# Three more Strassen units, a shared gather and a later first fold in a fused spectral and MLP kernel

## The chip, the cores and the metric

The kernel runs on one core of one Trainium2 chip. The metric is the device time of one execution in microseconds (us). An engine is named as the profile names it: PE is TensorE (PEld its weight loads), DVE is VectorE, ACT is ScalarE, POOL is GpSimd, SP is SyncE, which issues the DMAs.

## The reference

Input x is 2048 tokens of 448 features, all in float32. The output is a sum of three things: x, a spectral filter of the normalised x, and an MLP block with token shifts on the normalised x.

```python
def _A_ref(x, w_r, w_i):
    X = jnp.fft.rfft2(x, axes=(-2, -1)) * (w_r + 1j * w_i)
    return jnp.fft.irfft2(X, s=(S, D), axes=(-2, -1))

def _B_ref(x, w1, w2, w3, w4):
    h = _gelu(_layernorm(x, axis=-1) @ w1)        # 448 x 448
    # four quarters of h shifted by +1, -1, +2, -2 tokens, joined again
    x1 = x + shifted(h) @ w2                      # 448 x 448
    return x1 + _gelu(_layernorm(x1, axis=-1) @ w3) @ w4   # 448 x 1792, 1792 x 448

xn = _layernorm(A_x, axis=-1)
return A_x + _A_ref(xn, A_w_r, A_w_i) + _B_ref(xn, B_w1, B_w2, B_w3, B_w4)
```

## The kernel before

Every operand is split into a high and a low float16 part, and each product is three passes (high x high, high x low, low x high), named PASS. The 2048 tokens are 16 blocks of 128 (b = 0 to 15), kept in eight tiles xt of two blocks.

The first part of the kernel (up to about 100 us) normalises, multiplies by w1 and w2 and prepares w3 and w4. The rest consists of three kinds of work:

- The last two matrices, w3 and w4, run over eight groups of two blocks (G = 0 to 7) and seven units each (fp = 0 to 6, 256 hidden features a unit). `front` (matmuls on L384, tile pw) multiplies a unit by w3, 22 matmuls of 256 columns; ACT and DVE apply the gelu and split the result into tile hf (L704, L706, L707). `back` (L785, tile acc) multiplies it by w4, 12 matmuls of 448 columns, accumulated over the units of a group. L792 adds a finished accumulator to xt. `mlp` orders fronts and backs: a front runs one or two units ahead of its back.
- The spectral part: `do_fold` (L516 on ACT, L522 to L525 on POOL) and `step1` (L532, L533, PE on L542, tile ps) for every block; then 16 chunks (`chunk_a`, `chunk_b`, `chunk_z`, `chunk_c`: tiles pp, px, z, pu, PE on L600, L617, L645); then `gather_u` (L658), which copies the chunks' results Y1 into U for eight blocks at a time, four copies for the high and four for the low part; then `inv_a` (tile pe, L666) and `inv_b` (tile py, L687, L689) for every block.
- Units by Strassen's products. In groups 6 and 7, the units listed in SEVEN use seven products of half-size blocks (224 columns) in place of eight: `sums` makes the sums of the activations (tiles g and hz, L716 to L723), `w4_sums` those of w4 (L735, split by L267 and L268, into w4t), and `seven` issues 7 x 3 matmuls (L756) into the group's accumulators and two further PSUM banks, tile side. At the end of the group five DVE operations (L764) add the side banks to xt.

All of it is issued through a scheduling layer that orders the instructions of each engine by priority and by a modelled timeline. The groups are filler for the spectral part: groups 1 and 2 run beside the folds, 3 and 4 beside the chunks, 4 and 5 beside the inverse. Explicit ties hold some work behind other work: FOLD names, for each pair of blocks, the unit behind whose activation its fold stands on ACT, PACE the unit behind whose `back` the pair's step1 stands on PE, EARLY the units behind which the DMA and rescaling of earlier rows (`unscale`) are put, and LATE the units behind which the w4 sums stand.

PSUM tiles come from rotating pairs of banks by tag: mm for the fronts, acc for the accumulators, tr for pp and pe, sp for ps, px, pu and py. A tile must be read out before its bank is used again.

Of the kernel before, what the change touches and what calls it, by code (L numbers as in the profile page):

```python
# [15 lines left out]
AF = mybir.ActivationFunctionType  # L16
# [4 lines left out]
NB, NC = 16, 16  # L21
# [8 lines left out]
VPRE = 2.0 ** -3  # L30
EPS = 1e-5
AH = 2
PACE = [(0, 6), (1, 1), (1, 2), (1, 4), (1, 5), (2, 0), (2, 1), (2, 3)]
FOLD = [(0, 5), (1, 0), (1, 1), (1, 3), (1, 4), (1, 6), (2, 0), (2, 2)]
PIN = [("a3",), ("a3",), ("a3",), ("a3",)]
WMAX = [(1, 4), (1, 5), (1, 6), (2, 0), (2, 1), (2, 2), (2, 3), (2, 4)]
HS = 3
EVAC, FILL = 0, 100000
DH = D // 2
SEVEN = {6: [0, 1, 2, 3, 4, 5], 7: [0, 1, 2, 4, 5]}  # L40
ORD = {G: list(range(7)) for G in range(6)} | {6: list(range(7)), 7: [0, 1, 2, 4, 5, 3, 6]}

ME = [0, 224] + list(range(2, 224, 2))
MO = list(range(1, 224, 2))
# [78 lines left out]
def body(tc, nc, x, wf, w1, w2, w3, w4, c_g, c_n, c_small, out):  # L123
    V, A, P, T, SY = nc.vector, nc.scalar, nc.gpsimd, nc.tensor, nc.sync
    PSUM = bass.MemoryType.PSUM

    @contextlib.contextmanager
    def prio(base):
        kept = tc.cur_priority
        tc.cur_priority = max(base, at.get(base, 0))  # L130
        yield
        at[base] = tc.cur_priority
        tc.cur_priority = kept
# [19 lines left out]
    def bank(tag, name):  # L153
        return ps.tile([128, 512], F32, tag=tag, bufs=2, name=name)
# [106 lines left out]
    def split_w(hi, lo, src, s, low=None):  # L261
        if low is P:
            P.tensor_scalar(out=src, in0=src, scalar1=s, scalar2=0.0, op0=ALU.mult, op1=ALU.add)
            i = A.activation(out=hi, in_=src, func=AF.Copy)
            j = P.tensor_tensor(out=lo, in0=src, in1=hi, op=ALU.subtract)
            return i.ins, j.ins
        i = A.activation(out=hi, in_=src, func=AF.Copy, scale=s)  # L267
        j = V.scalar_tensor_tensor(out=lo, in0=src, scalar=s, in1=hi, op0=ALU.mult, op1=ALU.subtract)  # L268
        return i.ins, j.ins
# [88 lines left out]
    @contextlib.contextmanager  # L358
    def behind(*key):
        key = key if len(key) > 1 else key[0]  # L360
        with contextlib.ExitStack() as st:
            for i in after[key]:
                st.enter_context(tc.issue_after(i))
            yield
# [127 lines left out]
    def unscale(p, part):  # L492
        t = part.rearrange("p (b n) -> p b n", b=2)
        SY.dma_start(t, xv[:, 2 * p:2 * p + 2])
        return lambda: V.scalar_tensor_tensor(out=xt[p], in0=xt[p], scalar=p12, in1=t, op0=ALU.mult, op1=ALU.add)
# [14 lines left out]
    def do_fold(b0):  # L510
        X = pfd.tile([128, 2, D + 1], F32, tag="xf", bufs=3, name=f"xf{b0}")
        after["X", b0] = (SY.dma_start(X[:, :, 0:D], xv[:, b0:b0 + 2]).ins,)
        with behind("f", *FOLD[b0 // 2]):
            for i in range(2):
# [137 lines left out]
    U, vhs = {}, {}  # L652

    def gather_u(b0):
        U[b0] = [pv.tile([128, 4, 8, 128], F16, tag=f"U{p}", bufs=1, name=f"U{b0}{p}") for p in range(2)]
        for p in range(2):
            for q in range(4):
                V.tensor_copy(out=U[b0][p][:113, q].rearrange("p b (c k) -> p b c k", c=NC),  # L658
                              in_=Y1[:113, p, q, :, b0:b0 + 8].rearrange("p c b k -> p b c k"))

    def inv_a(b):
        pe = bank("tr", f"pe{b}")
# [29 lines left out]
    acc, hs = {}, {}  # L692

    def front(G, fp, tag):
# [5 lines left out]
        with prio(EVAC):  # L700
            if fp in SEVEN.get(G, ()):
                hs[G, fp] = sums(G, fp, pm)
# [24 lines left out]
    def w4_sums(j, part):  # L727

        t = part.rearrange("p (k n) -> p k n", n=DH)
        SY.dma_start(t.rearrange("p (f k) n -> p f (k n)", f=2), w4v[:, 2 * j:2 * j + 2])  # L730

        def go():
            for o, i, k, op in ((3, 3, 1, ALU.subtract), (1, 1, 0, ALU.subtract),
                                (0, 3, 0, ALU.add), (2, 2, 0, ALU.subtract)):
                V.tensor_tensor(out=t[:, o], in0=t[:, i], in1=t[:, k], op=op)  # L735
            split_w(w4t[j][:, 0], w4t[j][:, 1], t, s4)
        return go

    side = {}

    def seven(G, fp):
        h = hs.pop((G, fp))
        lead, last = fp == SEVEN[G][0], fp == SEVEN[G][-1]
        if lead:
            side[G] = [bank("sp" if G == 7 else "tr", f"side{G}{i}") for i in range(2)]
        m1, m6, m5, m7 = (side[G][i][:, DH * k:DH * k + DH] for i in range(2) for k in range(2))
        a2, a1 = acc[G][0], acc[G][1]
        a12 = acc[G][2][:, 0:DH] if G == 7 else a1[:, DH:D]
        w = lambda f, k: [w4p[0][:, i, 2 * fp + f, DH * k:DH * k + DH] for i in range(2)]
        t2, t1, t4, t3 = ([w4t[fp][:, i, k] for i in range(2)] for k in range(4))  # L750
        begins = fp == ORD[G][0]
        for blk, to, b, new in ((2, m1, w(0, 0), lead), (4, a1[:, 0:DH], w(1, 0), begins), (1, a2[:, 0:DH], t4, begins),
                                (6, a12, w(1, 1), begins and G == 7), (5, m5, t1, lead), (3, m6, t2, False),
                                (0, m7, t3, False)):
            for n, (hi, wi) in enumerate(PASS):
                m = T.matmul(to, h[:, hi, 128 * blk:128 * blk + 128], b[wi], start=new and n == 0,  # L756
                             stop=last and n == 2 and blk in (2, 5, 3, 0), skip_group_check=True)
        after["m", G, fp] = (m.ins,)
        if last:
            x = xt[G].rearrange("p b (k n) -> p (b k) n", k=2)  # L760
            wide = lambda m, n: m.unsqueeze(1).to_broadcast([128, n, DH])
            for to, m in ((x, wide(m1, 4)), (x[:, 0:2], wide(m6, 2)), (x[:, 3], m6), (x[:, 1:4:2], wide(m5, 2)),
                          (x[:, 0:2], wide(m7, 2))):
                V.scalar_tensor_tensor(out=to, in0=m, scalar=p34[:, 1:2], in1=to, op0=ALU.mult, op1=ALU.add)  # L764

    def back(G, fp):
        first, end = fp == ORD[G][0], fp == ORD[G][-1]
        if first:
            acc[G] = [bank("acc", f"acc{G}{i}") for i in range(2)]
            if G == 7:  # L770
                acc[G].append(bank("tr", "acc72"))
        if fp in SEVEN.get(G, ()):
            seven(G, fp)
            return
        h = hs.pop((G, fp))
        for i in range(2):
            b = 2 * G + i
            c = D // 2 if b == NB - 1 else D
            parts = [(slice(o, o + c), acc[G][i + o // c][:, 0:c]) for o in range(0, D, c)]
            for r, to in parts:  # L780
                with behind("m", G, fp) if G == 7 and end and ("m", G, fp) in after else contextlib.nullcontext():
                    for f in (2 * fp, 2 * fp + 1):
                        for n, (hi, wi) in enumerate(PASS):
                            o = 256 * (f % 2) + 128 * i
                            m = T.matmul(to, h[:, hi, o:o + 128], w4p[0][:, wi, f, r],  # L785
                                         start=first and f % 2 == 0 and n == 0, stop=end and f % 2 == 1 and n == 2,
                                         skip_group_check=G in SEVEN)
                after["m", G, fp] = (m.ins,)
            if end:
                with prio(EVAC):  # L790
                    for r, to in parts:
                        V.scalar_tensor_tensor(out=xb(b)[:, r], in0=to, scalar=p34[:, min(G, 1):min(G, 1) + 1],  # L792
                                               in1=xb(b)[:, r], op0=ALU.mult, op1=ALU.add)
                        if G > 4:
                            SY.dma_start(ov[:, b, r], xb(b)[:, r])

    def mlp(Gs, hook=None, ahead=1, tags=("mm",)):
        with prio(FILL):
            todo = [(G, fp) for G in Gs for fp in ORD[G]]
            done = 0  # L800
# [169 lines left out]
    Y1 = Y.rearrange("p i q c (b k) -> p i q c b k", k=8)  # L970
# [2 lines left out]
    for i in range(4):  # L973
        P.memset(xh_buf[i][:, 904:], 0.0)
    loads = stage("loads", 1808, 0)
    EARLY = {(1, 0): 1, (1, 1): 2, (1, 3): 3, (1, 5): 4, (1, 6): 5, (2, 1): 6, (2, 2): 7}

    def between(G, fp):
        if (G, fp) in EARLY:
            p = EARLY[G, fp]  # L980
            go = unscale(p, loads[:, 896 * (p % 2):896 * (p % 2) + 896])
            with behind("f", G, fp):
                go()

    mlp([1, 2], hook=between, ahead=AH, tags=("mm", "tr"))
    for b in range(0, NB, 2):
        do_fold(b)
        step1_in(b)
        step1_in(b + 1)
        with behind("m", *PACE[b // 2]):  # L990
            step1(b)
# [24 lines left out]
    for n in range(17):  # L1016
# [4 lines left out]
        if n:  # L1021
            b = bs[n - 1]
# [2 lines left out]
                finish(b)  # L1025
    close("pa2")
    pz = pool("pz")
    LATE = [(0, 5, 4), (1, 5, 5), (2, 5, 6), (3, 6, 0), (4, 6, 1), (5, 6, 3)]

    def w4_late(G, fp):  # L1030
        for n, (j, *at) in enumerate(LATE):
            if at == [G, fp]:
# [32 lines left out]
```

## Time and profile before

| | |
|---|---|
| median of 3 runs | 412.83 us (412.76 to 412.90) |
| the profiled execution | 412.93 us |
| its span, first to last instruction | 411.1 us |
| granted PE clock | 1.000 |
| PE matmul busy | 404.9 us, 98% of the span, 3382 matmuls |
| DVE busy | 329.5 us, 80% |
| ACT busy | 256.0 us, 62% |
| POOL busy | 96.8 us, 24% |
| DMA moved | 51.28 MB |

Busy time of PE is modelled at the matmuls' ends, so gaps between starts are the better measure. A row of the groups has: line, engine, operation, tiles written and read, shapes, count; then busy time in us and the mean of one in ns; then the engine's idle time before them and what ended it. A row of the timeline has: start in us from the span's start, length in us, engine, line, operation, tiles, count, and in brackets an idle time ahead of it with what ended it.

### The profile page before, as it was taken

How to read it: one execution, taken by the hardware profiler on the slowest of the kernel's cores; microseconds unless marked ns; L12 is line 12 of the kernel's file. 1: busy time of each engine (PE TensorE's matmuls, PEld its weight loads, DVE VectorE, ACT ScalarE, POOL GpSimd, SP SyncE). 2: the span in 40 equal slices, each digit the busy share in tenths (PEclk: the TensorE clock that was granted, in tenths of full speed). 3: DMA queues.
4: the chain of work that ended last, by engine and by line, in shares of the span. 5: the costliest groups of instructions: out<-in, count | busy, mean ns of one | idle time of the engine just before them, and what ended most of it. 6: DMA issues, size and time to landing. Idle time of an engine off the chain costs nothing.

```text
span 411.1 us, 8687 instructions
## 1 busy us (share of the span) xinstructions
PE 404.9 (98%) x3382; PEld 296.8 (72%) x3382; DVE 329.5 (80%) x675; ACT 256.0 (62%) x434; POOL 96.8 (24%) x172
## 2 busy tenths in 40 slices
PE   8999999999999999999999999999999999999996
PEld 3655555765658777777888887877776767998995
DVE  4888999898867879854798888967999978986645
ACT  4688879973757876544589887854344443653431
POOL 3877720101344947400022111110000000000000
PEclk9999999999999999999999999999999999999999
DMA  8959979914966557215256756510111043210101
GB/s 276 351 190 180 152 150 317 177 62 89 175 171 202 156 199 224 86 52 138 62 144 152 176 153 156 132 27 2 47 67 69 2 136 112 69 46 0 46 2 45
DMA packets 56168, 51.28 MB, mean 125 GB/s; under 512 B 37632, under 2 KB 50496, under 8 KB 56128
## 3 DMA queue, kind: packets, MB, share of 16 engines
q1 hardware_dynamic: 56128, 50.74, 46.6%
q8 instruction: 26, 0.43, 0.4%
q14 instruction: 14, 0.11, 0.1%
HBM read 38.28 MB, written 3.67 MB: 102 GB/s over the span
## 4 chain that ended last, share of the span: by engine, by line
PE 65%; DVE 13%; ACT 8%; issue 6%; DMA 5%; POOL 2%; SPq 1%; POOLq 0%; DVEq 0%; ACTq 0%
PE pw L384 26%; PE acc L785 19%; PE side L756 3%; PE ps L542 3%; PE pw L413 2%; PE pe L666 2%; PE acc L756 2%; PE py L687 2%; ACT te L622 2%; DVE xt L455 1%; PE pu L645 1%; DMA x2mem<-w 1%; PE pp L600 1%; DVE y L487 1%; PE px L617 1%
## 5 line engine op out<-in xcount | busy, mean ns | idle before, releaser
L384 PE MATMUL pw<-x2mem,w3p 128*128 128x256 f16 x1232 | 151.3, 273 | 0.0
L384 PEld LDWEIGHTS <-w3p 128*128 128x128 f16 x1232 | 119.2, 98 | 21.7
L785 PE MATMUL acc<-w4p,hf 128*128 128x448 f16 (+1 forms) x552 | 112.7, 348 | 0.6 <-DVE hf L707 0.6
L785 PEld LDWEIGHTS <-hf 128*128 128x128 f16 x552 | 53.5, 98 | 40.5 <-DVE hf L707 1.0
L704 ACT ACTIVATE pw<-pw,pe 128x512 f32<-128x512 f32 x45 | 29.4, 654 | 35.6 <-PE pw L384 35.4
L707 DVE SCALAR_TENSOR_TENSOR hf<-pw,h,hf 128x512 f16<-128x512 f32 x45 | 33.5, 746 | 15.2 <-ACT hf L706 14.9
L453 PE MATMUL pw<-w2p,h 112*128 112x448 f16 x192 | 39.9, 352 | 0.8 <-DMA h<-hs 0.8
L413 PE MATMUL pw<-w1p,xT 128*128 128x448 f16 x176 | 35.4, 352 | 0.0
L626 POOL TENSOR_TENSOR z<-te 128x450 f32<-128x450 f32 x16 | 15.7, 981 | 69.5 <-DVE te L624 69.5
L706 ACT ACTIVATE hf<-pw,h 128x512 f16<-128x512 f32 x45 | 30.7, 685 | 1.1
L453 PEld LDWEIGHTS <-h 112*128 112x128 f16 x192 | 18.7, 98 | 17.2 <-DMA h<-hs 1.0
L413 PEld LDWEIGHTS <-xT 128*128 128x128 f16 x176 | 17.0, 98 | 16.4 <-DVE xT L378 0.8
L607 ACT ACTIVATE pf<-pp 64x450 f16<-64x450 f32 x32 | 17.3, 542 | 12.6 <-DVE pf L608 8.3
L608 DVE TENSOR_TENSOR pf<-pp,pf 64x450 f16<-64x450 f32 x32 | 19.9, 622 | 4.3 <-ACT pf L607 3.9
L756 PEld LDWEIGHTS <-hz 128*128 128x128 f16 x231 | 22.2, 98 | 0.2
L722 ACT ACTIVATE hz<-g,h 128x896 f16<-128x896 f32 x11 | 11.5, 1041 | 14.3 <-DVE g L719 14.3
L622 ACT ACTIVATE te<-px 64x450 f32<-64x450 f32 x32 | 17.3, 539 | 1.1 <-PE px L617 0.6
L525 POOL TENSOR_TENSOR f<-xr 128x452 f32<-128x452 f32 x16 | 17.7, 1128 | 0.6
L533 DVE TENSOR_TENSOR xh<-f,xh 128x452 f16<-128x452 f32 x16 | 12.6, 829 | 5.5 <-ACT xh L532 5.5
L723 DVE SCALAR_TENSOR_TENSOR hz<-g,h,hz 128x896 f16<-128x896 f32 x11 | 12.6, 1150 | 5.1 <-ACT hz L722 4.9
L522 POOL TENSOR_TENSOR xr<-xf 128x452 f32<-128x452 f32 x8 | 9.4, 1179 | 25.9 <-issue 20.4
L532 ACT ACTIVATE xh<-f 128x452 f16<-128x452 f32 x16 | 8.4, 571 | 10.0 <-POOL f L525 10.0
(180 smaller groups left out, 688.4 us busy)
## 6 DMA issues: line engine op xcount, KB each, us to landing
wc<-wf SPq DMA_DIRECT2D x32, 225.0 KB, 3.8
wl<-wf SPq DMA_DIRECT2D x8, 450.0 KB, 3.7
xt<-x SPq DMA_DIRECT2D x8, 448.0 KB, 8.2
xf<-x SPq DMA_DIRECT2D x8, 448.0 KB, 3.7
loads<-x SPq DMA_DIRECT2D x7, 448.0 KB, 4.2
out<-xt SPq DMA_DIRECT2D x13, 224.0 KB, 1.9
w3raw<-w SPq DMA_DIRECT2D x3, 896.0 KB, 12.9
late<-w SPq DMA_DIRECT2D x6, 448.0 KB, 3.5
```

Source lines behind the costliest of these rows:

```text
L384: T.matmul(ps_out, wp[:, wi + t, cols], xT[:, xi + t, tok], start=t == 0 and wi + xi == 0, stop=t == 3 and wi == 4)
L413: T.matmul(pm[:, :D], xTs[g][:, xi + t, 128 * i:128 * i + 128], w1p[:, wi + t], start=t == 0 and p == 0, stop=t == 3 and p == 2)
L453: T.matmul(pm[:, :D], hT[g][:112, 4 * hi + k, o:o + 128], w2p[:, wi, k], start=n == 0, stop=n == 11)
L525: P.tensor_tensor(out=f[:, :, k:k + 2].rearrange("p b s d -> p s b d"), in0=u[:, :, 0], in1=u[:, :, 1], op=op)
L607: A.activation(out=hi, in_=src, func=AF.Copy)
L608: V.tensor_tensor(out=lo, in0=src, in1=hi, op=ALU.subtract)
L622: A.activation(out=e[64 * h:64 * h + 64], in_=px_[64 - 64 * h:128 - 64 * h, :2 * DF], func=AF.Copy)
L704: A.activation(out=pm, in_=pm, func=AF.Gelu_apprx_tanh, scale=r3)
L706: i = A.activation(out=h[:, 0], in_=pm, func=AF.Copy, scale=h3)
L707: j = V.scalar_tensor_tensor(out=h[:, 1], in0=pm, scalar=h3, in1=h[:, 0], op0=ALU.mult, op1=ALU.subtract)
L756: m = T.matmul(to, h[:, hi, 128 * blk:128 * blk + 128], b[wi], start=new and n == 0, stop=last and n == 2 and blk in (2, 5, 3, 0), skip_gr ...
L785: m = T.matmul(to, h[:, hi, o:o + 128], w4p[0][:, wi, f, r], start=first and f % 2 == 0 and n == 0, stop=end and f % 2 == 1 and n == 2, sk ...
```

## The change

Four things are changed.

1. `gather_u`: of the eight copies, those of the odd quarters are done by ACT, the others by DVE.
2. Three units of the sixth group (G = 5), numbers 0, 4 and 5, go by Strassen's products. The group's order becomes 1, 2, 3, 6, 0, 4, 5, and that of G = 6 becomes 0, 4, 5, 1, 2, 3, 6. `seven` can now be a group's last unit, so it takes `end` and `back` goes on to the readout after it. The side banks of G = 5 and 7 are of tag sp, those of G = 6 of tag tr.
3. The w4 sums for units 4, 5 and 0 are made beside groups 1 and 2 (behind units (2,3), (2,4), (2,5), through `between`); those for 1, 2 and 3 stay behind units of groups 5 and 6.
4. The first fold stands behind unit (0,6) instead of (0,5), and its step1 behind the back of (1,0) instead of (0,6).

```diff
-PACE = [(0, 6), (1, 1), (1, 2), (1, 4), (1, 5), (2, 0), (2, 1), (2, 3)]
-FOLD = [(0, 5), (1, 0), (1, 1), (1, 3), (1, 4), (1, 6), (2, 0), (2, 2)]
+PACE = [(1, 0), (1, 1), (1, 2), (1, 4), (1, 5), (2, 0), (2, 1), (2, 3)]
+FOLD = [(0, 6), (1, 0), (1, 1), (1, 3), (1, 4), (1, 6), (2, 0), (2, 2)]
...
-SEVEN = {6: [0, 1, 2, 3, 4, 5], 7: [0, 1, 2, 4, 5]}
-ORD = {G: list(range(7)) for G in range(6)} | {6: list(range(7)), 7: [0, 1, 2, 4, 5, 3, 6]}
+SEVEN = {5: [0, 4, 5], 6: [0, 4, 5, 1, 2, 3], 7: [0, 1, 2, 4, 5]}
+ORD = {G: list(range(7)) for G in range(5)} | {5: [1, 2, 3, 6, 0, 4, 5], 6: [0, 4, 5, 1, 2, 3, 6],
+                                               7: [0, 1, 2, 4, 5, 3, 6]}
...
-                V.tensor_copy(out=U[b0][p][:113, q].rearrange("p b (c k) -> p b c k", c=NC),
-                              in_=Y1[:113, p, q, :, b0:b0 + 8].rearrange("p c b k -> p b c k"))
+                to, of = U[b0][p][:113, q].rearrange("p b (c k) -> p b c k", c=NC), Y1[:113, p, q, :, b0:b0 + 8]
+                of = of.rearrange("p c b k -> p b c k")
+                if q % 2:
+                    A.activation(out=to, in_=of, func=AF.Copy)
+                else:
+                    V.tensor_copy(out=to, in_=of)
...
-            side[G] = [bank("sp" if G == 7 else "tr", f"side{G}{i}") for i in range(2)]
+            side[G] = [bank("tr" if G == 6 else "sp", f"side{G}{i}") for i in range(2)]
...
-                             stop=last and n == 2 and blk in (2, 5, 3, 0), skip_group_check=True)
+                             stop=n == 2 and (last if blk in (2, 5, 3, 0) else end), skip_group_check=True)
...
+        h = None
         if fp in SEVEN.get(G, ()):
-            seven(G, fp)
-            return
-        h = hs.pop((G, fp))
+            seven(G, fp, end)
+        else:
+            h = hs.pop((G, fp))
...
-            for r, to in parts:
+            for r, to in parts if h is not None else ():
...
-    EARLY = {(1, 0): 1, (1, 1): 2, (1, 3): 3, (1, 5): 4, (1, 6): 5, (2, 1): 6, (2, 2): 7}
+    EARLY = {(1, 0): 1, (1, 1): 2, (1, 3): 3, (1, 5): 4, (1, 6): 5, (2, 1): 6, (2, 2): 7,
+             (2, 3): "4", (2, 4): "5", (2, 5): "0"}
...
-            p = EARLY[G, fp]
-            go = unscale(p, loads[:, 896 * (p % 2):896 * (p % 2) + 896])
+            k, n = EARLY[G, fp], list(EARLY).index((G, fp))
+            part = loads[:, 896 * (n % 2):896 * (n % 2) + 896]
+            go = w4_sums(int(k), part) if isinstance(k, str) else unscale(k, part)
...
-    LATE = [(0, 5, 4), (1, 5, 5), (2, 5, 6), (3, 6, 0), (4, 6, 1), (5, 6, 3)]
+    LATE = [(1, 5, 0), (2, 5, 5), (3, 6, 4)]
```

More of the change, by code (lines that the diff above doesn't have):

```diff
@@ L739, in body, with seven @@
     side = {}
-    def seven(G, fp):
+    def seven(G, fp, end):
         h = hs.pop((G, fp))
```

## The prediction

> **What bounds the kernel now.** I read the page first, then the waits of TensorE (PE), the chain of waits, and the timeline around each place that the change touches. The page's first part, and all of PE's waits:
>
> ```profile
> PE 404.9 (98%) x3382; PEld 296.8 (72%) x3382; DVE 329.5 (80%) x675; ACT 256.0 (62%) x434; POOL 96.8 (24%) x172
> PE wps L815 <- DVE wsrc L186: 1.2, 1, 1.2
> PE pw L453 <- DMA h<-hs: 0.8, 1, 0.8
> PE acc L785 <- DVE hf L707: 0.6, 1, 0.6
> PE px L617 <- DVE te L623: 0.2, 1, 0.2
> ```
>
> PE waits four times in 411.1 us. So the time is the sum of PE's own spacings from one matmul to the next, and an edit counts only if it takes columns off PE, takes one of these waits away, or makes a new one. The chain of waits gives the spacings (start, us, what):
>
> ```profile
> 340.63 2.27 PE acc L785 x12
> ...
> 361.50 0.86 PE acc L756 x9
> 362.36 0.86 PE side L756 x9
> ```
>
> A 448-wide matmul takes 2.27 / 12 = 189 ns of PE, a 224-wide product 0.86 / 9 = 95.6 ns. PE is also the clock for all else: below I give each step's place by counting the matmuls ahead of it in the changed program's instruction order and multiplying by such spacings.
>
> **Three Strassen units.** An ordinary unit of the last matrix is 12 matmuls, 2.27 us. By Strassen it is 21 products, 21 x 95.6 ns = 2.01 us. Three units: 3 x 0.26 = **0.77 us off PE**, nearly certain, as PE waits for nothing near there. Each product needs its own weight load, 27 more in all; that these hide is shown by the 0.86 us rows, whose nine products had nine loads. Against this stands a rule of the Trainium skill ("TensorE: Matmul & The Clock Gate", Back-to-back issue gap): the spacing in a stream of load and matmul pairs comes from both, about 81 ns at 128 columns and 131 ns at 512. An estimate between these two figures of that page gives 94 ns at 224 and 123 ns at 448, so 1.96 us against 1.47 us, and three units would cost 1.5 us more. The rows above disagree at 448 columns (189 ns), and I go by them.
>
> **First fold one unit later.** This edit is small in the diff and worth as much. Timeline of before, start and us first:
>
> ```profile
> 112.83 1.41 ACT L516 ACTIVATE xf<-xf,nm,vw 128x448 f32<-128x448 f32 x2 [0.30 <-DMA xf<-x]
> 114.15 2.33 ACT L484 ACTIVATE y<-y,vs 128x448 f16<-128x448 f32 x4
> 114.84 0.29 DVE L485 SCALAR_TENSOR_TENSOR y<-y,vs 128x64 f16<-128x64 f32 x1 [1.52 <-ACT y L484]
> 116.66 1.36 POOL L522 TENSOR_TENSOR xr<-xf 128x452 f32<-128x452 f32 x1 [5.34 <-ACT xf L517]
> 118.03 1.43 DVE L487 SCALAR_TENSOR_TENSOR y<-y,vs 128x384 f16<-128x384 f32 x1
> 118.64 0.92 PE L785 MATMUL acc<-w4p,hf 128*128 128x448 f16 x4
> 119.38 0.74 DVE L707 SCALAR_TENSOR_TENSOR hf<-pw,h,hf 128x512 f16<-128x512 f32 x1
> 120.18 1.69 PE L785 MATMUL acc<-w4p,hf 128*128 128x448 f16 x8 [0.61 <-DVE hf L707]
> ```
>
> The first fold (L516) goes ahead of the four L484 on ScalarE (ACT), VectorE (DVE) waits for them, and its low half hf of unit (0,6) comes at 120.12. PE's four matmuls from 118.64 end at 118.64 + 4 x 0.189 = 119.40; the next starts at 120.18. That is 0.78 us lost, of which the waits view books 0.6. In the changed order the L516 pair stands behind this unit's own two activations. The L484 then start some 1.3 us earlier, DVE's four pairs follow by about 116.3, and hf is ready near 117.0, 1.4 us ahead of its first use; POOL's fold also no longer runs beside DVE's last pairs. So **0.77 us goes**, bounds 0.6 and 0.78. What is late next: the fold itself. Its four POOL steps took 116.66 to 121.24 and would take about 117.9 to 122.5, and ACT's L532 holds back the activation of unit (1,0) until 123.1; that unit's last-matrix matmuls come only after two more fronts, at about 127.5, and need it by 125.2 at the latest. I cost it at nothing; with that cover gone it would be a us.
>
> **w4 sums behind the third group.** Three sums move from the sixth and seventh group into units (2,3) to (2,5):
>
> ```profile
> L735 DVE TENSOR_TENSOR late<-late 128x224 f32<-128x224 f32 x24 | 9.0, 388 | 2.8 <-DMA late<-w 2.4
> L268 DVE SCALAR_TENSOR_TENSOR x2mem<-late,pe,x2mem 128x896 f16<-128x896 f32 x5 | 5.7, 1149 | 1.6 <-ACT x2mem L267 1.6
> L267 ACT ACTIVATE x2mem<-late,pe 128x896 f16<-128x896 f32 x5 | 5.1, 1038 | 3.9 <-DVE late L735 3.9
> late<-w SPq DMA_DIRECT2D x6, 448.0 KB, 3.5
> 180.00:190.00 10.00, 10.00 (x88) 7.46 (x87) 4.02 (x6) 3.88 (x6) 0.22 (x2) 1.00 0.05 9
> 190.00:200.00 10.00, 10.00 (x86) 6.61 (x85) 4.72 (x16) 4.81 (x9) 0.00 (x0) 1.00 0.59 151
> 188.26 1.15 SPq L588 DMA_DIRECT2D wc<-wf  x2
> 192.08 0.75 DVE L707 SCALAR_TENSOR_TENSOR hf<-pw,h,hf 128x512 f16<-128x512 f32 x1 [2.50 <-ACT hf L706]
> ```
>
> (The rows with colons are stretches: length, then busy us of PE, weight loads, DVE, ACT, POOL.) DVE gets 12 x 0.388 + 3 x 1.15 = 8.1 us more and ACT 3.1 us; DVE was free for 5.98 + 5.28 = 11.3 us of these 20. Queued behind: the third load can be issued only when the first sum is split (about 184.8 by DVE's order) and lands 3.5 us later, and DVE holds two L547 and the hf of unit (2,6) behind its subtraction. I get that hf at about 194.5 instead of 192.8. Its first use comes after 12 matmuls of unit (2,5), near 195.7, so 1.2 us hide it. On SP's queue the three loads stand ahead of the first wc loads; those started at 188.26, waiting for PE's last ps, later than 184.8. Cost: nothing, up to 1 us if the load lands 2 us late.
>
> **Gather half on ACT.**
>
> ```profile
> L658 DVE COPY U<-y 113x1024 f16<-113x1024 f16 x16 | 5.6, 420 | 0.0
> L532 ACT ACTIVATE xh<-f 128x452 f16<-128x452 f32 x16 | 8.4, 571 | 10.0 <-POOL f L525 10.0
> L517 ACT ACTIVATE xf<-xf 128x2 f32<-128x2 f32 x8 | 1.6, 199 | 0.1
> L241 ACT ACTIVATE xr<-w3raw 128x1792 f16<-128x1792 f32 x4 | 6.8, 1697 | 0.0
> 278.62 0.60 ACT L648 ACTIVATE y<-pu 113x512 f16<-113x512 f32 x1 [2.14 <-PE pu L645]
> 310.00:320.00 10.00, 10.00 (x89) 7.34 (x87) 9.89 (x26) 4.98 (x10) 0.00 (x0) 1.00 0.13 49
> ```
>
> DVE loses 8 x 0.35 = 2.8 us (5.6 / 16 each) where it is full (9.89 of 10). ACT gains eight copies. No row has this form; from L517 and L532 an element costs (571 - 199) / 450 = 0.83 ns, so 1024 of them 571 + 572 x 0.83 = 1.04 us; bounds 0.57 (the 452 row) and 1.70 (the 1792 row). I take 1.04, the same engine's slope. First gather: four copies and the L648 ahead of them end 0.2 + 0.6 + 4 x 1.04 = 5.0 us after the last pu matmul; in the changed order 5.9 us of matmuls stand between that and the first pe matmul that needs the fourth copy. Second: four copies and a vh activation, about 5.0 us, against 7.3 us. So both hide, down to a copy of (5.9 - 0.85) / 4 = 1.26 us. The gain on DVE is no gain in time, since PE did not wait.
>
> **What the Strassen units put on DVE and ACT.**
>
> ```profile
> L718 DVE TENSOR_TENSOR g<-g 128x256 f32<-128x256 f32 x11 | 4.6, 420 | 6.0 <-ACT g L716 6.0
> L719 DVE TENSOR_TENSOR g<-g 128x384 f32<-128x384 f32 x11 | 6.1, 555 | 0.2
> L723 DVE SCALAR_TENSOR_TENSOR hz<-g,h,hz 128x896 f16<-128x896 f32 x11 | 12.6, 1150 | 5.1 <-ACT hz L722 4.9
> L722 ACT ACTIVATE hz<-g,h 128x896 f16<-128x896 f32 x11 | 11.5, 1041 | 14.3 <-DVE g L719 14.3
> 400.56 3.74 DVE L764 SCALAR_TENSOR_TENSOR xt<-side,p,xt 128x896 f32<-128x896 f32 x5 [1.57 <-PE side L756]
> ```
>
> Per unit DVE does 0.42 + 0.56 + 1.15 instead of 0.74, so 3 x 1.39 = 4.2 us more, and 3.7 us of side sums once; the three sums that left give 8.1 us back. The totals cancel; the order matters. From a front's end to the low half it is about 4.4 us; the changed order leaves 5.5 to 7 us of matmuls. Two waits are new. The sixth group's side banks are the pair that py used, so the last L689 must have run: I place it at 0.9 us before the twelve side products that need it. And the accumulators pass to the seventh group only after side sums and L792 have been through DVE's queue: 0.3 us of room, and none for the low half of unit (6,5). I add 0.1 us for these; bounds 0 and 1.5.
>
> **Sum.** The profiled execution took 412.93 us (span 411.1 and 1.8 around it), 0.10 above the median of the three runs. 412.93 - 0.77 - 0.77 + 0.1 = 411.5; against the median of 412.83, **411.4**.
>
> **Rivals.** (1) The middle stage turns dearer. Its chunks are interleaved anew with groups four and five, and PE waited there once for DVE (0.2 us booked). A chunk now comes every 4.64 us of matmuls instead of 4.52, which speaks for fewer waits; where DVE is late for px or pu it is 0.2 to 0.4 us each. Four such give 412.2. (2) The handover to the seventh group binds: up to 1.5 us, 411.7 to 412.9. (3) Slower: ACT's copies with their short strided runs take twice the slope, 0.2 + 2 x 0.85 = 1.9 us. Then the first gather holds PE for 4 x (1.9 - 1.26) = 2.6 us and the second, with 1.7 us of room per copy, for 0.8: 414.8. It ends slower than before from about 1.8 us a copy on. For it: no row shows such a read on ACT. Against: the upper row is 1.70 for 1792 elements. The Trainium skill ("ScalarE: Activation LUTs", Rules for kernel authors) tells to keep simple element work on VectorE. An estimate by the formula in its section What ACT_TABLE_LOAD costs, 186 ns and 0.833 ns an element, is 1.04 us a copy, which agrees with the slope of the rows here. (4) The matmul rule told above: the units dearer instead of cheaper, by 3 x 0.49 us. From rows alone, if the products were spaced 120 ns each, the units would cost 3 x 0.25 us more and the sum would be 412.9; rows of 96 ns leave it 1 in 100.
>
> **How the numbers follow.** Forecast, both gains and no new wait over 0.3 us: 0.60 (410.9 to 411.8). Middle stage cheaper, its wait gone too: 0.07 (410.7). Rival 1: 0.15, rival 2: 0.11, each about half below 412.0. Rival 3: 0.05; rival 4 and the rest: 0.02. What a measurement tells from no change is about 0.2%, 0.83 us: faster is below 412.0, slower above 413.66. Faster: 0.60 + 0.07 + 0.12 = 0.79; slower 0.06 (rival 3 and a larger wait); same 0.15. The range takes in the cheaper case and most of rivals 1 and 2: 410.6 to 412.7.
>
> **What would show it.** Right: in the profile after, 231 + 63 products on the L756 line's successor at 96 ns, no wait of PE near 119 us, ACT copies near 1.04 us, and gaps of PE behind 175 us under 0.5 us in all. Wrong: PE waiting for ACT's U copies near 280 or 302 us, for DVE's hz or L792 between 338 and 362 us, or for px; each such wait would be in the waits of PE.

## The result, and the profile after

| | before | after |
|---|---|---|
| median | 412.79 us (412.41 to 413.35, 6 runs) | 411.01 us (410.80 to 412.19, 6 runs) |
| profiled execution, span | 412.93 us, 411.1 us | 410.80 us, 408.9 us |

The ratio is 0.9961, 95% interval 0.9948 to 0.9974: 1.8 us faster, 0.4 us more than forecast. Line numbers of after are one higher than before up to `gather_u`, five or six higher behind it.

The page's first part, and all that PE waits for in the profile after:

```profile
PE 403.6 (99%) x3409; PEld 299.4 (73%) x3409; DVE 329.1 (80%) x678; ACT 263.8 (65%) x442; POOL 96.3 (24%) x172
PE wps L821 <- DVE wsrc L187: 1.2, 1, 1.2
PE pw L454 <- DMA h<-hs: 0.7, 1, 0.7
```

Of the four waits of before two are left, both of the first 35 us. The wait for hf near 119 us is gone, and so is the one for px near 252 us, which the forecast's sum had left standing. DVE's total is the same within 0.4 us and ACT has 7.8 us more: what moved lies beside PE's work.

The gather, by the groups; the last number ahead of the bar's end is the mean of one copy in ns:

```profile
L662 ACT ACTIVATE U<-y 113x1024 f16<-113x1024 f16 x8 | 7.9, 1046 | 0.4 <-PE pe L671 0.4
L664 DVE COPY U<-y 113x1024 f16<-113x1024 f16 x8 | 2.9, 427 | 0.0
```

A copy takes 1.046 us on ACT, as the slope of the other rows gave (1.04), and 0.36 us of DVE's time (2.9 / 8).

The place of the first fold, timeline of after:

```profile
112.71 2.34 ACT L485 ACTIVATE y<-y,vs 128x448 f16<-128x448 f32 x4
115.88 0.61 DVE L488 SCALAR_TENSOR_TENSOR y<-y,vs 128x384 f16<-128x384 f32 x1
116.21 1.41 ACT L517 ACTIVATE xf<-xf,nm,vw 128x448 f32<-128x448 f32 x2
116.41 0.75 DVE L712 SCALAR_TENSOR_TENSOR hf<-pw,h,hf 128x512 f16<-128x512 f32 x1
118.18 0.92 PE L791 MATMUL acc<-w4p,hf 128*128 128x448 f16 x4
...
119.04 1.68 PE L791 MATMUL acc<-w4p,hf 128*128 128x448 f16 x8
...
122.06 1.05 ACT L533 ACTIVATE xh<-f 128x452 f16<-128x452 f32 x2 [4.21 <-POOL f L526]
```

The activations L485 now come first, at 112.71 instead of 114.15 us. DVE's last L488 takes 0.61 us; before, beside POOL's fold, the same operation took 1.43, and the L485 of before ahead of it 1.08 instead of 0.28:

```profile
117.02 1.08 DVE L485 SCALAR_TENSOR_TENSOR y<-y,vs 128x64 f16<-128x64 f32 x1
```

So about half of what hf gains is ACT's order and about half the work that DVE no longer does beside POOL. The hf is done at 116.41 + 0.75 = 117.16, 1.9 us ahead of the matmuls at 119.04, which carry no wait. The fold's own step ends at 123.1, as foreseen.

### The profile page after: what moved, and what is told of

Read it like the earlier page. It is cut to its first block, busy times and chain, and to the rows that moved or that the text cites. A ratio compares the mean times of both kernels' runs of the same rounds, so it can differ in the third digit from the quotient of the medians.

```text
span 408.9 us, 8753 instructions
## 1 busy us (share of the span) xinstructions
PE 403.6 (99%) x3409; PEld 299.4 (73%) x3409; DVE 329.1 (80%) x678; ACT 263.8 (65%) x442; POOL 96.3 (24%) x172
## 4 chain that ended last, share of the span: by engine, by line
PE 91%; POOL 5%; issue 2%; DMA 1%; ACT 0%; DVE 0%; POOLq 0%
PE pw L385 33%; PE acc L791 23%; PE pw L454 9%; PE pw L414 4%; PE side L761 4%; PE acc L761 3%; PE pu L646 3%; PE ps L543 3%; PE pp L601 2%; PE pe L671 2%; PE px L618 2%; PE py L692 2%; POOL xt L323 1%; DMA h<-hs 1%; POOL w2s L264 1%
## 5 line engine op out<-in xcount | busy, mean ns | idle before, releaser
L385 PEld LDWEIGHTS <-w3p 128*128 128x128 f16 x1232 | 119.3, 98 | 20.5
L791 PE MATMUL acc<-w4p,hf 128*128 128x448 f16 (+1 forms) x516 | 105.1, 348 | 0.0
L791 PEld LDWEIGHTS <-hf 128*128 128x128 f16 x516 | 49.8, 98 | 36.5
L709 ACT ACTIVATE pw<-pw,pe 128x512 f32<-128x512 f32 x42 | 27.4, 653 | 33.3 <-PE pw L385 33.3
L712 DVE SCALAR_TENSOR_TENSOR hf<-pw,h,hf 128x512 f16<-128x512 f32 x42 | 31.3, 748 | 17.2 <-ACT hf L711 17.0
L711 ACT ACTIVATE hf<-pw,h 128x512 f16<-128x512 f32 x42 | 28.7, 686 | 1.0
L761 PEld LDWEIGHTS <-hz 128*128 128x128 f16 x294 | 28.2, 98 | 0.5
L727 ACT ACTIVATE hz<-g,h 128x896 f16<-128x896 f32 x14 | 14.6, 1043 | 15.6 <-DVE g L724 15.6
L728 DVE SCALAR_TENSOR_TENSOR hz<-g,h,hz 128x896 f16<-128x896 f32 x14 | 16.1, 1150 | 6.7 <-ACT hz L727 6.7
L721 ACT ACTIVATE g<-pw,pe 128x512 f32<-128x512 f32 x14 | 9.6, 688 | 17.5 <-PE pw L385 15.9
L798 DVE SCALAR_TENSOR_TENSOR xt<-acc,p,xt 128x448 f32<-128x448 f32 (+1 forms) x17 | 10.9, 653 | 5.9 <-PE acc L791 5.7
```

The costliest lines, as they stand in the source:

```text
L385: T.matmul(ps_out, wp[:, wi + t, cols], xT[:, xi + t, tok], start=t == 0 and wi + xi == 0, stop=t == 3 and wi == 4)
L709: A.activation(out=pm, in_=pm, func=AF.Gelu_apprx_tanh, scale=r3)
L711: i = A.activation(out=h[:, 0], in_=pm, func=AF.Copy, scale=h3)
L712: j = V.scalar_tensor_tensor(out=h[:, 1], in0=pm, scalar=h3, in1=h[:, 0], op0=ALU.mult, op1=ALU.subtract)
L791: m = T.matmul(to, h[:, hi, o:o + 128], w4p[0][:, wi, f, r], start=first and f % 2 == 0 and n == 0, stop=end and f % 2 == 1 and n == 2, sk ...
```

## Where the 2 us came from

In the trace's records I take the time from the start of the first L785 matmul to the start of the last (L791 after; the line of the same statement in the other kernels). It leaves out the start of the kernel and the last output DMA, which differ from one execution to the next. It names what each part is worth better than the medians do:

| kernel | first to last, us | median, us | ratio to before |
|---|---|---|---|
| before; once more | 313.48; 313.54 | 412.79 to 413.36 | 1 |
| changed; once more | 311.47; 311.48 | 411.01; 411.19 | 0.9961; 0.9959 |
| fold alone | 312.71 | 412.11 | 0.9978 |
| gather alone | 314.88 | 414.39 | 1.0031 |
| units and sums, no fold, no gather | 312.97 | 412.13 | 0.9980 |
| changed, ordinary units | 312.25 | 411.67 | 0.9970 |
| changed, gather on DVE | 311.50 | 410.97 | 0.9950 |

Before to fold alone: -0.77, with the wait near 119 us as these two executions of before have it (it can be larger, see the last experiment). Fold alone to the changed kernel with ordinary units (sums and gather added): -0.46. From there to the changed kernel (units added): -0.78. Together -2.01. The rest of the spans' 2.26 us is the first part of the kernel, which the change doesn't touch: the first L785 came at 94.03 us in the profile of before and at 93.79 after, and at 93.8 to 94.1 in all the executions below.

## The experiments

**The parts one by one.** These four kernels ran on one chip, beside the kernel before. First the fold alone, in the kernel before:

```diff
-PACE = [(0, 6), (1, 1), ...
-FOLD = [(0, 5), (1, 0), ...
+PACE = [(1, 0), (1, 1), ...
+FOLD = [(0, 6), (1, 0), ...
```

> The kernel before with the fourth part of the change alone: the first fold stands behind unit (0,6), its step1 behind the back of (1,0). PE's instruction order behind 200 us is then that of before. Theory (the fold's term of the sum was right, and the middle stage's gain belongs to another part): 0.77 us less than before, a ratio of 0.9981; PE's wait for hf near 119 us is gone, the gaps ahead of px near 252 and 262 us (0.33 and 0.15 us) stay. Rival A (the later fold also frees the middle stage): 1.25 us less, 0.9970, with these two gaps gone as well. Rival B (the fold is late for unit (1,0)): a new PE wait of up to 1 us near 125 us and a ratio of 0.999 or more.

Measured: 412.11 us against 413.01, ratio 0.9978 (0.9969 to 0.9986). The profile's waits of PE:

```profile
PE wps L815 <- DVE wsrc L186: 1.2, 1, 1.2
PE pw L453 <- DMA h<-hs: 0.8, 1, 0.8
PE px L617 <- DVE te L623: 0.2, 1, 0.2
```

The hf wait is gone, the px wait stays, and the gaps at 251.1 and 261.6 us are 0.33 and 0.15 us as before. The theory holds; neither rival shows.

The gather alone, in the kernel before:

```diff
-                V.tensor_copy(out=..., in_=...)
+                if q % 2:
+                    A.activation(out=to, in_=of, func=AF.Copy)
+                else:
+                    V.tensor_copy(out=to, in_=of)
```

> The kernel before with the first part of the change alone: of the eight copies of a gather the odd quarters go to ACT. Theory (a copy of 1.05 us hides, and what DVE is spared is not on the path): the time of before within 0.2 us, ratio 0.9995 to 1.0005. In this order the second gather leaves ACT's fourth copy about 4.95 us of PE work, against 0.2 + 0.6 + 4 x 1.05 = 5.0 us, so a PE wait of up to 0.1 us near 307 us may show. Rival A (the gather's share of DVE held up the late stage): 0.3 us or more less. Rival B (the copies hold PE): 0.3 us or more longer, booked to ACT near 281 or 307 us.

Measured: 414.39 us, ratio 1.0031 (1.0019 to 1.0043). The theory fell, to rival B. Timeline of this kernel at the second gather:

```profile
302.87 3.90 ACT L661 ACTIVATE U<-y 113x1024 f16<-113x1024 f16 x4 [0.98 <-PE pe L670]
306.68 0.59 ACT L674 ACTIVATE e<-pe 128x226 f32<-128x226 f32 x2
307.36 0.38 DVE L678 TENSOR_TENSOR e<-pe,e 128x226 f32<-128x226 f32 x1
307.80 1.46 PE L670 MATMUL pe<-csm,U 113*128 113x113 f16 x24 [0.55 <-DVE e L678]
```

PE does not wait for the copies; it waits for a bank of pe. The readout e of the last two pe stands behind the four copies in ACT's queue, so DVE frees the bank only at 307.74. The gap there is 0.71 us, with smaller ones 0.91 us. The scheduling layer answered the edit with another order of PE behind 283 us, so this is the price of the copies in the order that they came with, not in that of before to the letter. The other 0.49 us of the longer span is a larger hf wait near 119 us (below). In the changed order the same readout is just as late, but the next pe is not due yet:

```profile
305.83 1.04 ACT L662 ACTIVATE U<-y 113x1024 f16<-113x1024 f16 x1
306.78 0.34 ACT L675 ACTIVATE e<-pe 128x226 f32<-128x226 f32 x1
309.70 0.77 PE L671 MATMUL pe<-csm,U 113*128 113x113 f16 x12
```

From 306.78 the bank is free some 1.1 us later, near 307.9, and PE comes at 309.70: 1.8 us of room.

Units and sums without fold and gather: the changed kernel with

```diff
-PACE = [(1, 0), ...
-FOLD = [(0, 6), ...
+PACE = [(0, 6), ...
+FOLD = [(0, 5), ...
...
-                if q % 2:
-                    A.activation(out=to, in_=of, func=AF.Copy)
-                else:
-                    V.tensor_copy(out=to, in_=of)
+                V.tensor_copy(out=..., in_=...)
```

> The changed kernel without the first and fourth parts: the gather is all on DVE and the first fold stands where it stood; the units and the w4 sums are as changed. PE's order of the middle stage is that of the changed kernel, with a px of chunk 13 and 14 standing otherwise than before. Theory (the units are worth 0.77 us, and the w4 sums, by the new order, take the 0.48 us of gaps out of the middle stage): 1.25 us less than before, 0.9970; the hf wait near 119 us is there, no px wait near 252 us. Rival A (the middle stage's gain came from the fold or the gather): 0.77 us less, 0.9981, with the px gaps still there. Rival B (the units need the gather's relief on DVE): a PE wait for hz, py or the accumulators behind 335 us, and a ratio above 0.9985.

Measured: 412.13 us, ratio 0.9980 (0.9970 to 0.9990), between the theory and rival A. The trace tells why: no px gap, no wait behind 335 us, but the hf wait near 119 us was larger than in the profile of before. Its gap was 1.46 us instead of 0.78, and 313.48 - 0.77 - 0.48 + 0.68 = 312.91 against 312.97 measured. So the theory's parts hold and the size of the hf wait does not.

The changed kernel with ordinary units:

```diff
-SEVEN = {5: [0, 4, 5], 6: ...
+SEVEN = {6: ...
-ORD = ... 5: [1, 2, 3, 6, 0, 4, 5], ...
+ORD = ... 5: list(range(7)), ...
```

> The changed kernel with ordinary matmuls for the sixth group's three units (its order of units is 0 to 6 again); the gather, the early w4 sums and the fold are as changed, and PE's order up to the sixth group is that of the changed kernel. Theory (units worth 0.77 us; fold 0.77; middle stage 0.48 by the early sums): 1.25 us less than before, 0.9970, so 0.77 us more than the changed kernel. By an estimate from the Trainium skill (TensorE: Matmul & The Clock Gate, Back-to-back issue gap), in which a Strassen unit is dearer than an ordinary one, it would be 1.5 us faster than the changed kernel. Rival (the middle stage's gain hangs on the units): no px gain, 0.77 us less than before, 0.9981.

Measured: 411.67 us, ratio 0.9970 (0.9958 to 0.9981), 0.78 us more than the changed kernel from first to last L785 matmul. The theory holds. The px gaps are gone without the units, so they went with the sums: PE's order in the middle stage is one in all kernels with these three early sums, and the one of before in all kernels without; the two part at 191 us, where the last of these sums is made. That the late groups' new order of units did it can be ruled out: the changed kernel and this one differ in that order and agree on PE up to 330 us, and kernels below with four and five units, which have the same early sums, agree up to 316. The rows are the px near 252 us and DVE's read of the px ahead of it, in the profile of before and then of after:

```profile
251.54 0.69 DVE L623 SCALAR_TENSOR_TENSOR te<-px,sc,wc 128x450 f32<-128x450 f32 x1 [0.19 <-ACT te L622]
252.29 0.74 PE L617 MATMUL px<-pf,gn 128*128 128x225 f16 x6 [0.17 <-DVE te L623]
```

```profile
250.83 0.69 DVE L624 SCALAR_TENSOR_TENSOR te<-px,sc,wc 128x450 f32<-128x450 f32 x1 [0.17 <-ACT te L623]
252.16 0.74 PE L618 MATMUL px<-pf,gn 128*128 128x225 f16 x6
```

Before, the px comes 0.06 us after DVE has read the last px out of the bank; after, 0.64 us after. Nobody meant this: eight us of DVE's work were moved, and the scheduling layer, which fits each engine's order to a modelled timeline, put the chunks elsewhere between the fillers. That the new order has fewer gaps is luck.

**The gather on either engine, and the changed kernel again.** These kernels, and the first with four units in the next part, ran on a second chip, again beside the kernel before.

> The changed kernel once more, beside the three kernels of this group on one chip. Theory: 411.0 us, ratio to before 0.996; PE's spacings beyond the plain ones come to 6.3 us again (7.8 before), none of it near 119, 252 or 262 us. Rival: the earlier execution was a lucky one, and a gap of 0.1 us or more shows behind 110 us.

Measured: 411.19 us, ratio 0.9959 (0.9946 to 0.9971); no gap over 0.1 us behind 110 us. From 35 us on, the spacings exceed the median of their form by 0.7 us in sum, as in the first execution (0.7; before 2.0). The sum over the whole kernel, on which the theory put 6.3 us, hangs on the few matmuls of the start and says nothing here. The first execution was no accident.

The changed kernel with all copies on DVE (edit as above):

> The changed kernel with the whole gather on DVE as before; all else as changed. Theory (in the changed order the gather is hidden on either engine): the time of the changed kernel within 0.2 us, as the kernel with units and sums but without gather and fold had no PE gap over 0.12 us behind 280 us. Rival A (the change needs ACT's help, since DVE is full there): a PE wait for hf, e or vh between 280 and 340 us and 0.3 us or more longer. Rival B (ACT's copies cost a little, as they did alone in the order of before, where they cost 0.9 us near 307 us): 0.3 us or more shorter than the changed kernel.

Measured: 410.97 us, ratio 0.9950 (0.9937 to 0.9962), 0.03 us more from first to last L785 matmul. PE waits for nothing behind 35 us. The theory holds: beside the other parts, the first part of the change is worth nothing, either way. The two kernels' orders of PE part at 285 us, so it is two plans of the scheduling layer, each with its gather, that take the same time.

All eight copies on ACT:

```diff
-                if q % 2:
+                if q >= 0:
```

> The changed kernel with all eight copies of a gather on ACT. It tests the price that the rival on ACT's copies was worked out by: a copy of 1.05 us, hidden until the matmul that needs it. First gather: the third pe matmul needs the fifth copy, which ends 0.2 + 0.6 + 5 x 1.05 = 6.1 us after the last pu matmul, and the order leaves 4.7 us, so PE waits 1.4 us near 284 us; the matmuls behind have more room. Second gather: the fifth copy is through after 5.5 us and a vh, and the order leaves 9.8 us: no wait there. Theory: 1.4 us more than the changed kernel (412.4). Rival A (ACT's gelu and e activations queued behind eight copies hold PE as well): 2.5 us more or worse, with PE waits for hf or e. Rival B (the copies hide all the same): 0.2 us or less.

Measured: 416.50 us, ratio 1.0080 (1.0067 to 1.0094), 5.3 us more than the changed kernel. Rival A, and worse. Two places, by the timeline, and the stretches around the second (length, busy us of PE, weight loads, DVE, ACT, POOL, then the granted clock):

```profile
280.52 7.68 ACT L662 ACTIVATE U<-y 113x1024 f16<-113x1024 f16 x8
288.11 1.21 ACT L709 ACTIVATE pw<-pw,pe 128x512 f32<-128x512 f32 x2
289.25 0.59 ACT L675 ACTIVATE e<-pe 128x226 f32<-128x226 f32 x2
290.38 0.78 PE L671 MATMUL pe<-csm,U 113*128 113x113 f16 x12 [1.65 <-DVE e L679]
...
354.77 1.04 DVE L769 SCALAR_TENSOR_TENSOR xt<-side,p,xt 128x448 f32<-128x448 f32 x2
355.72 1.14 DVE L728 SCALAR_TENSOR_TENSOR hz<-g,h,hz 128x896 f16<-128x896 f32 x1
...
356.92 0.37 PE L761 MATMUL side<-w4p,hz 128*128 128x224 f16 x1 [1.95 <-DVE hz L728]
```

```profile
350.00:354.00 4.00, 4.00 (x43) 3.92 (x41) 3.16 (x6) 1.26 (x2) 0.00 (x0) 1.00 0.04 12
354.00:357.00 3.00, 1.01 (x9) 0.50 (x8) 3.00 (x6) 2.33 (x4) 0.00 (x0) 0.96 0.54 153
357.00:360.00 3.00, 3.00 (x17) 2.34 (x18) 3.00 (x5) 1.27 (x2) 0.00 (x0) 0.50 0.00 0
360.00:364.00 4.00, 4.00 (x38) 3.64 (x37) 4.00 (x10) 0.79 (x1) 0.00 (x0) 0.98 0.26 102
```

At 288.6 PE loses 1.8 us, and again not for a copy (the expected 1.4 us) but for a bank of pe, whose readout e stands on ACT behind eight copies and behind the two L709 activations of a front that the copies held up. At 354.8 PE idles 2.1 us for hz: its low half (L728) stands on DVE behind two side sums (L769). The order planned with eight copies differs here too: its last py matmul comes at 349.6 us, in the changed kernel at 338.4, so the inverse's work on DVE reaches further into the sixth group. That this is what delays hz is likely, not shown. Behind the idle time the clock is 0.50 for 3.4 us, matmuls of 224 columns are spaced 187 ns, and this costs 1.6 us more.

**More units.** Four instead of three (the sums of unit 1 behind (2,6), the order 2, 3, 6, 0, 4, 5, 1):

```diff
-SEVEN = {5: [0, 4, 5], ...
+SEVEN = {5: [0, 4, 5, 1], ...
-             (2, 3): "4", (2, 4): "5", (2, 5): "0"}
+             (2, 3): "4", (2, 4): "5", (2, 5): "0", (2, 6): "1"}
-    LATE = [(1, 5, 0), (2, 5, 5), (3, 6, 4)]
+    LATE = [(2, 5, 0), (3, 6, 4)]
```

> The changed kernel with a fourth unit of the sixth group, number 1, by Strassen's products; its w4 sums are made behind unit (2,6), and the group's order is 2, 3, 6, 0, 4, 5, 1. Theory (a unit is worth 0.26 us wherever its sums are hidden): 0.26 us less than the changed kernel, 410.75. Rival A (the side banks are py's, and the lead unit now comes 4.4 us sooner: the side products stand right behind the last py in PE's order): a PE wait of 0.3 to 1.5 us near 345 us for DVE's readout of py, 411.0 to 412.2. Rival B (a fourth sum behind the third group holds hf of (3,0)): a PE wait near 200 us of up to 1 us.

Measured: 412.08 us, ratio 0.9977 (0.9967 to 0.9987), 0.9 us slower than the changed kernel: rival A, and more. Timeline:

```profile
344.67 0.45 PE L761 MATMUL side<-w4p,hz 128*128 128x224 f16 x3 [0.21 <-DVE xt L694]
346.95 1.04 ACT L268 ACTIVATE x2mem<-late,pe 128x896 f16<-128x896 f32 x1 [4.85 <-DVE late L740]
347.89 1.96 ACT L727 ACTIVATE hz<-g,h 128x896 f16<-128x896 f32 x2
348.98 0.36 PE L761 MATMUL side<-w4p,hz 128*128 128x224 f16 x2 [0.69 <-ACT hz L727]
```

0.37 us go to the bank that py still holds (L694 reads it), 0.86 us to hz, which stands on ACT behind the split of a w4 sum (L268) that itself waits for DVE (L740), and 0.16 us right behind it. These 1.4 us less 0.26 for the unit are 1.14; first to last L785 matmul it is 312.63, 1.15 more than the changed kernel.

So I turned the side banks round (tag tr, pe's pair, for the sixth and eighth group), with the gather on DVE, first with three units:

```diff
-            side[G] = [bank("tr" if G == 6 else "sp", ...
+            side[G] = [bank("sp" if G == 6 else "tr", ...
-                acc[G].append(bank("tr", "acc72"))
+                acc[G].append(bank("sp", "acc72"))
```

> The changed kernel with the gather on DVE, and with the side banks the other way round: those of the sixth and eighth group of tag tr (the pair that pe uses), those of the seventh, and the eighth's third accumulator, of tag sp. Theory (with three units no side product waits, on either pair of banks): 411.0 us, the time of the changed kernel within 0.2 us, and no PE gap over 0.1 us behind 200 us. Rival A (the handover of the banks to the seventh and eighth group binds this way round): a PE wait for xt or side behind 355 us, 0.3 us or more longer. Rival B (py's banks cost the changed kernel something that the view of waits does not book): 0.2 us or more shorter.

Measured: 410.76 us, ratio 0.9942 (0.9929 to 0.9955), first to last 311.50 as with the other banks: the theory. (The median lies 0.2 us lower than with the other banks, within the intervals of the two; PE's records show nothing of it.) Then with four units:

> The kernel with four units in the sixth group again, now with the gather on DVE and the side banks of tag tr, so that the side products stand in front of the last two py instead of right behind the last. Theory (the four units lost their 0.26 us, and more, to py's readout and to the order behind it): no gap at the side products, 0.26 us less than the changed kernel, 410.75. Rival A (DVE has no room for a fourth unit's sums while the inverse runs: the 0.86 us wait for hz stays): 411.4 to 412.0, with a PE wait for hz near 340 to 350 us. Rival B (pe's readout takes the place of py's): a PE wait for e near 338 us.

Measured: first to last 311.24, 0.26 us less than with three units and no gap behind 200 us, which is the theory. In the median, 411.14 us (ratio 0.9955, 0.9939 to 0.9970), the gain is not to be seen: the runs lie between 410.60 and 412.64, and in the profiled one, of 412.64, the last output DMAs took 4.0 us from issue to landing, against 1.8 in the profiled executions of all other kernels:

```profile
out<-xt SPq DMA_DIRECT2D x2, 112.0 KB, 4.0
```

And with five units:

```diff
-SEVEN = {5: [0, 4, 5, 1], ...
+SEVEN = {5: [0, 4, 5, 1, 2], ...
-ORD = ... 5: [2, 3, 6, 0, 4, 5, 1], ...
+ORD = ... 5: [3, 6, 0, 4, 5, 1, 2], ...
-    LATE = [(2, 5, 0), (3, 6, 4)]
+    LATE = [(2, 5, 6), (3, 6, 4)]
```

> Five units of the sixth group by Strassen's products (0, 4, 5, 1, 2; the group's order is 3, 6, 0, 4, 5, 1, 2), the gather on DVE and the side banks of tag tr; the w4 sums of unit 2 are made behind unit (5,6). Theory (each unit is worth 0.26 us as long as its sums are hidden): the last matmul 0.26 us sooner than with four units and 0.5 us sooner than with three, and 410.5 us. Rival (two units earlier their sums fall into the inverse, where DVE is full): PE waits for hz, vh or py between 320 and 350 us, 0.3 us or more in all, and the time of three units or more.

Measured: 410.74 us, ratio 0.9946 (0.9932 to 0.9959), first to last 311.33. The fifth unit's 0.26 us went into one new gap of 0.33 us, where DVE has two L724 in a row:

```profile
365.14 2.21 DVE L724 SCALAR_TENSOR_TENSOR hz<-g,h,hz 128x896 f16<-128x896 f32 x2 [3.06 <-ACT hz L723]
366.35 0.27 PE L757 MATMUL side<-w4p,hz 128*128 128x224 f16 x1 [0.16 <-DVE hz L724]
```

All three are faster than the kernel before; that one of them is faster than the changed kernel was not shown.

**The wait near 119 us, once more in the kernel before.**

> The kernel before once more, to see the gap near 119 us a further time. So far it was 0.78 us in the profile of before, 1.27 and 1.46 us in two kernels whose program is the same up to there. Theory (ACT's and DVE's work ahead of it starts when the DMAs of y into x2mem have landed, so its length differs from execution to execution): between 0.6 and 1.6 us, the longer the later the second pair of that DMA lands; the rest of PE's gaps behind 40 us as before within 0.1 us. Rival (the gap is fixed by the program): 0.78 us again within 0.05.

Measured: 412.91 us, the gap 0.83 us, all else as before. By itself this doesn't part the theory from its rival. The four executions with the old fold do:

| execution | second L475 pair of ACT starts | hf of (0,6) done | gap of PE |
|---|---|---|---|
| before | 110.60 | 120.12 | 0.78 |
| before again | 110.54 | 120.08 | 0.83 |
| units and sums | 110.97 | 120.59 | 1.46 |
| gather alone | 111.19 | 120.68 | 1.27 |

hf comes 9.5 to 9.6 us after that activation starts in all four, and PE's last matmul ahead of it starts between 119.0 and 119.3; so the gap has no fixed size. In the gather's execution the activation waits for the DMA that reads y, in the others the profile names DVE:

```profile
111.19 0.67 ACT L475 ACTIVATE y<-xt,nm 128x448 f32<-128x448 f32 x1 [1.88 <-DMA x2mem<-y]
```

That the DMA's landing makes the difference each time is thus likely, not shown. With the fold one unit later the hf is 1.9 us early, and the spread is hidden. The spans from first to last instruction fit this: with the old fold they lie between 410.3 and 411.8 us in the 23 runs of before beside the first experiments, and between 409.0 and 410.5 in the 12 with units and sums; with the later fold between 408.8 and 409.3 in the eleven runs of the changed kernel, and between 410.1 and 410.7 in the eleven with the fold alone. The times themselves spread further: one run of the changed kernel took 412.19 us with a span of 409.1.

## Why the prediction was right

- **What bounds the kernel.** Right: PE's spacings and its few waits gave every difference above to within 0.1 us.
- **Units, -0.77.** Measured -0.78, with 294 products at 96 ns. The rule of the Trainium skill (TensorE: Matmul & The Clock Gate, Back-to-back issue gap), by which load and matmul together set the spacing and the units would have cost 1.5 us, does not hold here. What that section gives for an isolated matmul, N / 2.4 + 2.5 ns, an estimate of 96 ns at 224 and 189 at 448 columns, agrees with both rows.
- **Fold, -0.77.** Measured -0.77 against the profile of before, the execution that the figure was read from. In others the old place lost up to 1.46 us, so that the mechanism is shown, the exact match is luck, and the bounds of 0.6 and 0.78 were too narrow. Medians give -0.90 (-0.6 to -1.3).
- **w4 sums at no cost.** Right as to their own place: the third set of sums was done early enough that hf of (2,6) came at 193.1, not 194.5 as I had it. But the sum left out what they did elsewhere: the middle stage lost its gaps, 0.48 us. I had this case at 0.07 and the opposite, rival 1, at 0.15, although I had noted that chunks at 4.64 us speak for fewer waits. This is the term that was mis-sized, and the largest part of what the time beat the forecast by. So what came is, by its mechanism, the case of 0.07 (410.7); that the measured 411.01 also lies in the interval of the main forecast (410.9 to 411.8) is luck.
- **Gather.** The result (nothing) was right, the working was not. The break-even of 1.26 us a copy looked at the matmul that reads the copies. What binds first is the readout of pe that is queued behind them on ACT; I had counted one vh there and no e. In the kernel with the gather alone that cost 0.9 us with copies of the same length, and with eight copies it came to 1.8 us at the first gather. It hides in the changed kernel because the next pe happens to come 1.8 us after its bank is free; that the gather costs nothing is luck of the order, not the margin that was worked out.
- **Strassen's load on DVE and ACT, +0.1.** Measured 0. The side products had 1.7 us of room, not 0.9, and the accumulators' handover 1.8 us, not 0.3:

```profile
339.21 0.68 DVE L694 SCALAR_TENSOR_TENSOR xt<-py,sc,xt 128x448 f32<-128x448 f32 x1
341.56 1.31 PE L761 MATMUL side<-x2mem,hz 128*128 128x224 f16 x12
354.07 0.69 DVE L798 SCALAR_TENSOR_TENSOR xt<-acc,p,xt 128x448 f32<-128x448 f32 x1
356.51 0.74 PE L761 MATMUL acc<-x2mem,hz 128*128 128x224 f16 x6
```

- **Rivals.** 2 and 4 did not come. Rival 3 was wrong in its cause (the copies take 1.046 us), but near in kind: a slower gather on ACT does end on the other side, by the pe banks.
- **The sum.** The profiled time came out 0.7 us under the 411.5: 0.48 the middle stage, 0.1 the allowance, 0.24 the earlier start, less 0.13 outside the span.

## What to carry to other kernels

Where PE is never idle, an edit is worth its columns and the waits that it removes, and both can be read to a tenth of a microsecond from one trace, but the size of a wait can be that of one execution (0.78 to 1.46 us here): take several before you price it. When work moves to another engine, price everything queued behind it there, above all the readouts that free PSUM banks, and not only its own consumer. Where a scheduling layer re-plans all engines, a part that is harmless in one order can cost in another, so judge parts in the order that they will run in, and give the waits of other stages a term in the sum.

## What had not been expected of the hardware

With eight copies on ACT, PE stood idle for 2.1 us (354.8 to 356.9) and then ran at a granted clock of 0.50 until 360.2; 3.4 us at half speed turned a 2.1 us wait into 3.7. The idle time of 1.8 us at 288.6 in the same execution was followed by a clock of 1.00. It may not come every time: of the four runs of this kernel three have a mean clock of 0.996 and spans of 414.6 to 415.0 us, the fourth 1.000 and 413.2, but only one of the four, with 0.996, left a trace. The Trainium skill (TensorE: Matmul & The Clock Gate, Part 1: The HAM clock gate) has half rate follow an idle window of some 3.4 us, and a busy window of that length bring full speed back. The length of the slow stretch agrees; that it takes an idle time of a whole window does not, as 2.1 us were enough here. What decides between 1.8 and 2.1 us, the length or the moment, no run here shows.
